# A gated recurrence followed by a rational MLP: the third pair of token groups loaded whole and turned by TensorE, with a new table of steps

## The chip, the cores and the metric

One core of a Trainium2 chip runs the whole program. The metric is the device time of one execution in microseconds (us); several executions of a kernel are timed and their median is given. A profile is one further look at one of these executions, taken by the hardware profiler. The engines are TensorE (PE in the profile; its loading of weights is PEld), VectorE (DVE), ScalarE (ACT), GpSimd (POOL) and SyncE (SP), which here only issues DMAs.

## The reference

For each of 4 batches and 8 heads there is a sequence of 768 tokens of 48 values, and a state of 48x48 that decays by `alpha` and takes up an outer product:

```python
for t in range(S):
    state = alpha[:, :, t, :, None] * state + np.einsum('bhd,bhe->bhde', k[:, :, t], v[:, :, t])
    y[:, :, t] = np.einsum('bhd,bhde->bhe', q[:, :, t], state)
x = y.transpose(0, 2, 1, 3).reshape(B * S, H * D)      # 3072 tokens of 384
h = x @ w_in                                            # 384 -> 2048
g = (a[0] + a[1]*h + a[2]*h**2 + a[3]*h**3) / (1 + |b[0]|*|h| + |b[1]|*h**2 + 1e-6)
out = g @ w_out                                         # 2048 -> 384
```

## The kernel before

**The recurrence.** The 768 tokens of a batch are worked in six groups of 128, so there are 24 groups, numbered g through all batches. Two neighbouring groups are a pair m. For each group the running products of `alpha` along the tokens are made by VectorE as two scans (`suffix` L462, `prefix` L474), k and q are multiplied by them (`mult_k` L483, `mult_q` L486, on GpSimd or VectorE), TensorE makes scores (`sc_mm` L504), turns k (`k_turn` L537), makes the products for the state (`kv_mm` L568) and the output of the group (`attn_mm` L586); GpSimd masks the scores (`sc_mask` L531) and decays the state (`decay` L556). The scans need channels on the partitions and tokens along the row, while memory holds tokens by rows, so alpha, k and q have to be turned. There are two ways of doing it.

- Groups 0 to 3 (pairs 0 and 1, `NNAT = 2`): `load_nat` (L408) loads alpha, k or q of a whole pair in one DMA of 384 KB, `turn_nat` (L425) turns it on TensorE by sixteen transposes into PSUM, and `copy_nat` (L444) has ScalarE copy it from there to where the group wants it.
- Groups 4 to 23: `load_akq` (L401) loads 48 KB at a time, 24 DMAs to a group, and VectorE turns them in 32x32 blocks (`turn_a` L454, `turn_qk` L459).

**The MLP.** Its work is cut into 96 units u: the first 8 with whole f32 weights (`plain_in` L668, `plain_out` L681), the rest as "wide" units of 128 hidden channels by 512 tokens, where weights and data are split in a high and a low part (`wide_in` L695, `wide_out` L714, and L708 for the last 512 tokens). Each unit passes through ScalarE (L750, L753, L780, L783, L799), VectorE (L773, L777, L787, L790, L796) and GpSimd (L762, L803, and L757 where ScalarE's L759 does not do that step). The weights come as 64-bit words; in the first part of the program sixteen pieces of them are brought to f32 by `join_scale` (L270, ScalarE or GpSimd), `join_low` (L278, VectorE), `join_sign` (L282 on ScalarE or L284 on VectorE) and `join` (L298, VectorE), and split by L313 and L318.

**The order.** Every step is declared once with `add(key, engine, ..., after=[...])`, the engine it runs on, an `alt` engine for some, and the steps that must stand ahead of it. `Plan.run` then issues the steps in the order of the table `ORDER`, a packed list of step numbers; the top bit of a number says that the step runs on its `alt` engine. So one table sets the order on all engines and on the DMA queue of SP, and who does the steps that two engines can do. `warm` (L418) is a row of transposes at the start that write nothing of use. At the end `last_done` (L741, L743) copies the last 512 tokens' results from PSUM in pieces of 128 tokens, and `last_store` (L747) stores them; the last 128 tokens are cut in two halves of columns, one for VectorE and one for ScalarE.

## Time and profile before

| what | us |
|---|---|
| median of 3 executions | 530.17 (528.98 to 531.47) |
| the profiled execution's own time | 531.47 |
| its span, first to last instruction | 529.4 |
| busy in the span: PE / DVE / ACT / POOL | 501.9 / 494.2 / 459.1 / 423.5 |
| PE instructions / DMA packets | 5082 / 145656 |
| mean granted TensorE clock | 0.988 of full |

The profiled execution is the longest of the three; its span leaves out 2.07 us that lie around it. A busy share here is the mean over two quite different parts: a beginning in which data and weights are prepared on all engines, and a long remainder in which the units follow each other. They have to be read apart.

### The profile page before, as it was taken

How to read it: one execution, taken by the hardware profiler on the slowest of the kernel's cores; microseconds unless marked ns; L12 is line 12 of the kernel's file. 1: busy time of each engine (PE TensorE's matmuls, PEld its weight loads, DVE VectorE, ACT ScalarE, POOL GpSimd, SP SyncE). 2: the span in 40 equal slices, each digit the busy share in tenths (PEclk: the TensorE clock that was granted, in tenths of full speed). 3: DMA queues.
4: the chain of work that ended last, by engine and by line, in shares of the span. 5: the costliest groups of instructions: out<-in, count | busy, mean ns of one | idle time of the engine just before them, and what ended most of it. 6: DMA issues, size and time to landing. Idle time of an engine off the chain costs nothing.

```text
span 529.4 us, 13659 instructions
## 1 busy us (share of the span) xinstructions
PE 501.9 (95%) x5082; PEld 411.9 (78%) x5082; DVE 494.2 (93%) x773; ACT 459.1 (87%) x805; POOL 423.5 (80%) x421
## 2 busy tenths in 40 slices
PE   7865988987999999999999999999999999999996
...
GB/s 262 248 250 268 155 197 88 106 152 132 127 144 117 89 105 100 97 99 94 119 86 116 111 91 100 83 113 32 120 83 130 47 2 41 0 61 59 2 2 63
DMA packets 145656, 56.81 MB, mean 107 GB/s; under 512 B 133424, under 2 KB 138160, under 8 KB 145584
## 3 DMA queue, kind: packets, MB, share of 16 engines
...
HBM read 47.98 MB, written 4.72 MB: 100 GB/s over the span
## 4 chain that ended last, share of the span: by engine, by line
PE 81%; ACT 6%; DVE 4%; SPq 4%; DMA 3%; issue 1%; POOL 1%; DVEq 0%; POOLq 0%
PE ps L695 34%; PE ps L714 28%; PE ps L708 6%; PE ps L586 4%; PE ps L681 2%; PE ps L504 2%; PE ps L568 2%; SPq L408 2%; PE ps L537 1%; DMA wi_words<-in_moe_w_in_dram 1%; ACT wo_words L282 1%; DMA wo_words<-in_moe_w_out_dram 1%; PE ps L668 1%; SPq L448 1%; SPq L401 1%
## 5 line engine op out<-in xcount | busy, mean ns | idle before, releaser
L695 PE MATMUL ps<-x,wi 128*128 128x512 f32 x792 | 204.4, 398 | 1.7 <-DVE t L796 1.7
L695 PEld LDWEIGHTS ps<-x,wi 128*128 128x128 f32 x792 | 146.5, 188 | 34.7 <-DVE t L796 2.7
L714 PE MATMUL ps<-gh_gl,wo 128*128 128x512 f32 x648 | 170.2, 399 | 0.2 <-ACT gh_gl L799 0.2
L714 PEld LDWEIGHTS ps<-gh_gl,wo 128*128 128x128 f32 x648 | 119.1, 188 | 27.2 <-ACT gh_gl L799 0.6
L762 POOL TENSOR_TENSOR qm<-qm,ah 128x512 f32<-128x512 f32 x96 | 124.2, 1294 | 14.8 <-ACT qm L759 5.9
L803 POOL TENSOR_TENSOR gh_gl<-t,gh_gl 128x512 fp32r<-128x512 f32 x83 | 108.6, 1309 | 16.3 <-ACT gh_gl L799 11.8
L753 ACT ACTIVATE t<-ps,coef 128x512 f32<-128x512 f32 x96 | 74.7, 778 | 6.9 <-PE ps L695 4.8
L787 DVE SCALAR_TENSOR_TENSOR t<-t,coef,ps 128x512 f32<-128x512 f32 x96 | 70.7, 737 | 6.5 <-ACT ps L783 5.1
L780 ACT ACTIVATE ps<-qm,one_eps 128x512 f32<-128x512 f32 x96 | 66.4, 691 | 11.5 <-DVE t L777 6.1
L750 ACT ACTIVATE ah<-ps 128x512 f32<-128x512 f32 x96 | 57.0, 594 | 20.6 <-PE ps L695 19.4
L777 DVE SCALAR_TENSOR_TENSOR t<-t,coef,ps 128x512 f32<-128x512 f32 x96 | 70.9, 739 | 1.0
L757 POOL TENSOR_SCALAR qm<-ah,bab 128x512 f32<-128x512 f32 x61 | 47.9, 786 | 28.6 <-ACT ah L750 16.8
L773 DVE TENSOR_TENSOR t<-t,ps 128x512 f32<-128x512 f32 x96 | 64.9, 677 | 4.6 <-ACT t L753 2.9
L796 DVE SCALAR_TENSOR_TENSOR t<-ps,t 128x512 f32<-128x512 f32 x96 | 65.6, 683 | 1.1
L790 DVE SCALAR_TENSOR_TENSOR ps<-qm,ps 128x512 f32<-128x512 f32 x96 | 65.9, 687 | 0.2
L783 ACT ACTIVATE ps<-ps 128x512 f32<-128x512 f32 x96 | 56.1, 585 | 2.0
L799 ACT ACTIVATE gh_gl<-t 128x512 fp32r<-128x512 f32 x88 | 55.1, 627 | 3.0 <-DVE t L796 2.8
L531 POOL TENSOR_SCALAR_AFFINE_SELECT tqk<-tqk 64x512 f32<-64x512 f32 x48 | 33.1, 690 | 13.9 <-ACT tqk L525 7.6
L486 POOL TENSOR_TENSOR tqk<-tqk,fp 128x512 f32<-128x512 f32 x22 | 28.9, 1312 | 8.9 <-DVE wi_words L298 7.7
L462 DVE TENSOR_TENSOR_SCAN tg<-ta,ps 128x528 f32<-128x528 f32 x24 | 29.7, 1242 | 6.6 <-ACT ta L444 6.5
L586 PEld LDWEIGHTS ps<-tqk,sv 128*32 128x32 f32 x1536 | 23.4, 112 | 15.1 <-POOL tqk L531 7.1
L483 POOL TENSOR_TENSOR tqk<-tqk,tg 128x512 f32<-128x512 f32 x23 | 30.4, 1322 | 5.6 <-ACT tqk L444 5.3
(112 smaller groups left out, 728.8 us busy)
## 6 DMA issues: line engine op xcount, KB each, us to landing
raw_a<-in_alpha_dram SPq DMA_DIRECT2D x160, 48.0 KB, 2.2
...
```

The lines of the kernel that those rows point to most:

```text
L695: nc.tensor.matmul(h_of(u), w(key)[:, kt * FU + f % FU, :], x[:, kt, xp, :], start=(n == 0), stop=(n == len(todo) - 1),)
L714: nc.tensor.matmul(bank(O_BANKS[dt]), w(("o", f // FU))[:, f % FU, dt * P : (dt + 1) * P], g, start=(f == 0 and first_w), stop=(f == NF - ...
L750: nc.scalar.activation(buf(s, "ah", u), h_of(u), AF.Abs)
L753: nc.scalar.activation(buf(s, "t1", u), h_of(u), AF.Identity, bias=a2, scale=a3)
L762: nc.gpsimd.tensor_tensor(buf(s, "qm", u), buf(s, "qm", u), buf(s, "ah", u), op=ALU.mult)
L773: nc.vector.tensor_tensor(t, t, h_of(u), op=ALU.mult)
L777: nc.vector.scalar_tensor_tensor(t, t, a1, h_of(u), op0=ALU.add, op1=ALU.mult)
L780: nc.scalar.activation(h_of(u), buf(s, "qm", u), AF.Abs_reciprocal_sqrt, bias=one_eps)
L787: nc.vector.scalar_tensor_tensor(t, t, a0, h_of(u), op0=ALU.add, op1=ALU.mult)
L790: nc.vector.scalar_tensor_tensor(h_of(u), buf(s, "qm", u), 1.0 + 1e-6, h_of(u), op0=ALU.add, op1=ALU.mult)
L796: nc.vector.scalar_tensor_tensor(t, h_of(u), 2.0, t, op0=ALU.subtract, op1=ALU.mult, reverse0=True)
L803: eng.tensor_tensor(buf(s, "gl", u).rearrange("p a b -> p (a b)"), buf(s, "t1", u), gh, op=ALU.subtract)
```

## The change

The third pair (groups 4 and 5) goes the way of the first two: `NNAT = 3`. Its alpha is loaded into the buffer that pair 0 used and its k and q into a buffer of their own (`nat_raw`), and its transposes write to PSUM bank 4 (`SCB`), which the recurrence uses as well, so they may only stand between two groups (`NAT_AFTER`: alpha behind group 2, k and q behind group 3), and one half of a pair's tensor has to be copied out before the next is turned. Since the buffers are shared, the small loads of alpha of group 6 wait for the turning of the third pair's alpha. `warm` is two products of 128x512 in place of twenty transposes. The last 128 tokens are copied by ScalarE in one piece and stored by one DMA that ScalarE issues. The table `ORDER` is another one throughout, and with it the engine of some sixty of the steps that two engines can do.

```diff
--- before.py
+++ after.py
@@ -70,70 +70,70 @@
 
 
 ORDER = [
-    'c-jTQ1E3u`3;@t3X_~gPZQHhO+qS*k?fK2NZQHhO+xFi-XN*!Rx^gOtLN!)RQeLr&t;VUzDykZ<jGCubs3|I%TBxR~`D&t',
+    'c-jru1A`sR4gk<eGRdH}ZQHhO+qT==-R-KjZQHhO+qS>HcmBmuDyl-|R2;=BiW;M0t4V6C8m~loHBK#8Q`IUpMa5FlR7^E',
...
 ]
@@ -148,8 +148,9 @@
     (0, "a"): (0, 1), (0, "k"): (4, 5), (0, "q"): (6, 7),
     (1, "a"): (0, 1), (1, "q"): (6, 7), (1, "k"): (2, 6),
 }
-NNAT = 2
-WARM = 20
+NNAT = 3
+NAT_AFTER = {"a": 2, "k": 3, "q": 3}
+WARM = 2
 WB = 2
 GB = 3
 NSC = 1
@@ -406,16 +407,22 @@
     def load_nat(m, nm):
         b, sg = divmod(m, NSEG)
         nc.sync.dma_start(
-            raw[nm][m][:, 0 : H * 2 * D].rearrange("p (h w) -> p h w", h=H),
+            raw[nm][nat_raw(m, nm)][:, 0 : H * 2 * D].rearrange("p (h w) -> p h w", h=H),
             SRC[nm][b, :, sg * SEG : (sg + 1) * SEG, :].rearrange("h (p t) d -> p h (t d)", t=2),
         )
 
     def nat_bank(m, nm, par):
-        return NAT_BANKS[m, nm][par]
+        return NAT_BANKS[m, nm][par] if (m, nm) in NAT_BANKS else SCB
+
+    def nat_raw(m, nm):
+        return m if m < 2 else 0 if nm == "a" else 2
 
     def warm():
         for n in range(WARM):
-            nc.tensor.transpose(bank(2, P), ident, ident)
+            nc.tensor.matmul(
+                bank(2).rearrange("p (a b) -> p a b", b=P), ident, ident.unsqueeze(1).to_broadcast([P, BANK // P, P]),
+                start=True, stop=True,
+            )
 
     def turn_nat(m, nm, par):
         for a in range(NPAIR):
@@ -423,7 +430,7 @@
                 c0 = 2 * D * (2 * a + j) + D * par - DP * j
                 w = DP * (j + 1)
                 nc.tensor.transpose(
-                    bank(nat_bank(m, nm, par))[0:w, a * C : (a + 1) * C], raw[nm][m][:, c0 : c0 + w], ident
+                    bank(nat_bank(m, nm, par))[0:w, a * C : (a + 1) * C], raw[nm][nat_raw(m, nm)][:, c0 : c0 + w], ident
                 )
 
     def turned(nm, g):
@@ -735,16 +742,16 @@
                 parts[32 * a : 32 * (a + 1), dt * SUP : (dt + 1) * SUP].rearrange("j (c i) -> j c i", i=32),
             )
 
-    def last_done(eng, tt, c0, c1):
-        o, x = parts[:, tt * DM + c0 : tt * DM + c1], bank(T_BANKS[tt], DM)[:, c0:c1]
+    def last_done(eng, tt):
+        o = parts[:, tt * DM : (tt + 1) * DM]
         if eng is nc.scalar:
-            eng.activation(o, x, AF.Copy)
+            eng.activation(o, bank(T_BANKS[tt], DM), AF.Copy)
         else:
-            eng.tensor_copy(o, x)
-
-    def last_store(eng, tt, c0, c1):
+            eng.tensor_copy(o, bank(T_BANKS[tt], DM))
+
+    def last_store(eng, tt):
         r = (NSUP - 1) * SUP + tt * P
-        eng.dma_start(out[r : r + P, c0:c1], parts[:, tt * DM + c0 : tt * DM + c1])
+        eng.dma_start(out[r : r + P, :], parts[:, tt * DM : (tt + 1) * DM])
 
     def act_ah(u, s):
         nc.scalar.activation(buf(s, "ah", u), h_of(u), AF.Abs)
@@ -962,7 +969,7 @@
     add("ident", "POOL", 0.5, make_identity, (nc, ident))
     add("coef", "SP", 2 * DMA, load_coef, kb=0.1)
     if WARM:
-        add("warm", "PE", 0.11 * WARM, warm, (), ["ident"], lat=0.13)
+        add("warm", "PE", 0.93 * WARM, warm, (), ["ident"], lat=0.13)
     add("bab", "ACT", 0.2, abs_coef, (), ["coef", "prime"])
     add("floor_s", "POOL", 0.1, nc.gpsimd.memset, (floor_s, FLOOR))
     add("one_eps", "POOL", 0.1, nc.gpsimd.memset, (one_eps, 1.0 + 1e-6))
@@ -1003,15 +1010,27 @@
 
     NGC = 2 * NBLK
     nat_users = [[] for _ in range(8)]
+    def cps(m, nm, par=(None, 0, 1)):
+        return [("cp", m, nm, p, cc) for p in par for cc in range(2)]
+
+    def group_done(g):
+        return [(x, g) for x in ("xh", "xl", "km", "kv")] + [("se", g, 0), ("se", g, 1)]
+
     for m in range(NNAT):
-        for nm in "aqk":
-            add(("nat", m, nm), "SP", DMA, load_nat, (m, nm), (), kb=1.45)
+        late = []
+        for nm in "aqk" if m < 2 else "akq":
+            add(("nat", m, nm), "SP", DMA, load_nat, (m, nm), [("tn", 0, nm, par) for par in range(2)] if m == 2 and nm == "a" else (), kb=1.45)
             for par in range(2):
-                b = nat_bank(m, nm, par)
-                before = [("cp", *x, p, cc) for x in nat_users[b] for p in (None, 0, 1) for cc in range(2)]
-                nat_users[b].append((m, nm))
+                if m < 2:
+                    b = nat_bank(m, nm, par)
+                    before = [y for x in nat_users[b] for y in cps(*x)]
+                    nat_users[b].append((m, nm))
+                else:
+                    before = late + group_done(NAT_AFTER[nm]) + [("kt", NAT_AFTER[nm]), ("s", NAT_AFTER[nm]), ("vk", NAT_AFTER[nm]), ("am", NAT_AFTER[nm])]
+                    late = cps(m, nm, (par,))
+                set_k = ("set", "k", nat_raw(m, "k"))
                 add(("tn", m, nm, par), "PE", 0.9, turn_nat, (m, nm, par),
-                    [("nat", m, nm), ("set", nm, m), "ident", "warm"] + before + ([("nat", m, "k"), ("set", "k", m)] if nm == "q" else []), lat=0.13)
+                    [("nat", m, nm), ("set", nm, nat_raw(m, nm)), "ident", "warm"] + before + ([("nat", m, "k"), set_k] if nm == "q" else []), lat=0.13)
     for g in range(NGC):
         m, cc = divmod(g, 2)
         old = [(w, g - NQ) for w in ("am", "s", "kt")]
@@ -1026,7 +1045,7 @@
                 ready[nm] = [("cp", m, nm, par, cc) for par in pairs]
             else:
                 for qd in range(4):
-                    ov = [("tn", 0, x, p) for p in range(2) for x in ("a" if nm == "a" else "kq") if nm == "a" or raw_at(g) == 0]
+                    ov = [("tn", y, x, p) for y in (0, 2) for p in range(2) for x in ("a" if nm == "a" else "kq") if nat_raw(y, x) == (0 if nm == "a" else raw_at(g))]
                     add(("ld", nm, g, qd), "SP", 2 * DMA, load_akq, (nm, g, qd), [("ta", g - 1) if nm == "a" else ("tqk", g - 2), ("set", nm, 0 if nm == "a" else raw_at(g))] + ov, kb=0.23)
         if m >= NNAT:
             add(("ta", g), "DVE", 0.71, turn_a, (g,), [("ld", "a", g, qd) for qd in range(4)] + into["a"])
@@ -1043,7 +1062,8 @@
             add(("sv", g, c), "SP", DMA, load_sv, (g, c), [("set", "v", g % NV), ("am", g - NV), ("vk", g - NV)], kb=0.9)
     for g in range(NGC):
         near = [("cp", *x, p, cc) for b in (SCB, SCB + 1) for x in nat_users[b] for p in (None, 0, 1) for cc in range(2)]
-        was = [("xh", g - 1), ("xl", g - 1), ("km", g - 1), ("kv", g - 1), ("se", g - 1, 0), ("se", g - 1, 1)]
+        was = group_done(g - 1)
+        near += [y for nm in "akq" if NAT_AFTER[nm] == g - 1 for y in cps(2, nm, (0, 1))]
         add(("kt", g), "PE", 0.38, k_turn, (g,), [("k", g)] + was + near, lat=0.13)
         add(("ke", g), "ACT", 0.55, k_evac, (g,), [("kt", g), ("vk", g - NSC), "set_st"])
         add(("s", g), "PE", SV[0], sc_mm, (g,), [("k", g), ("q", g), ("ke", g)] + was + near, lat=0.13)
@@ -1127,12 +1147,9 @@
                     old = [("ws", m - 1, dt) for dt in range(KT)]
                     add(("og", tt), "PE", 0.35, last_out, (u, tt, "gh"), [("gh", u), ("lo", ("o", j))] + prev, due=at)
                     add(("ot", tt), "PE", 0.175, last_out, (u, tt, "gl"), [("og", tt), ("ot", tt - 1), ("gl", u)], lat=0.13, due=at + 2)
-                    cut = DM // 2 if tt == PER - 1 else DM
-                    for c0 in range(0, DM, cut):
-                        part = (m, tt, c0) if c0 else (m, tt)
-                        act = c0 > 0 or tt == 1
-                        add(("wd", *part), "ACT" if act else "DVE", 0.5 if cut == DM else 0.33, last_done, (nc.scalar if act else nc.vector, tt, c0, c0 + cut), [("ot", tt)] + old, due=at + 3)
-                        add(("ws", *part), "ACT" if c0 else "SP", DMA, last_store, (nc.scalar if c0 else nc.sync, tt, c0, c0 + cut), [("wd", *part)], kb=0.55 * cut / DM)
+                    act, own = tt % 2, tt == PER - 1
+                    add(("wd", m, tt), "ACT" if act else "DVE", 0.5, last_done, (nc.scalar if act else nc.vector, tt), [("ot", tt)] + old, due=at + 3)
+                    add(("ws", m, tt), "ACT" if own else "SP", DMA, last_store, (nc.scalar if own else nc.sync, tt), [("wd", m, tt)], kb=0.55)
                 continue
             add(("oh", u, 0), "PE", WIDE * KT, wide_out, (u, hi, "gh"), [("gh", u), ("lo", ("o", j)), ("ol", u - 1), ("oh", u - 1, 1)] + old, due=at)
             add(("oh", u, 1), "PE", WIDE * KT, wide_out, (u, lo, "gh"), [("oh", u, 0)], due=at + 1)```

**GpSimd, groups 2 and 3, at the first units.** `tqk_88` to `tqk_90` are the buffers of turned k and q of three groups in a row: L483 and L486 with `tqk_90` and the masking with `tqk_90` belong to group 2, those with `tqk_88` to group 3; `qm` is a unit's. Before:

```order
L483 TENSOR_TENSOR tqk_90<-tqk_90,tg_86 128x512
L486 TENSOR_TENSOR tqk_88<-tqk_88,fp_85 128x512
L762 TENSOR_TENSOR qm_103<-qm_103,ah_98 128x512
L483 TENSOR_TENSOR tqk_88<-tqk_88,tg_87 128x512
L556 TENSOR_TENSOR sv_91<-st_s,tots_94 48x4x48
L556 TENSOR_TENSOR sv_91<-st_s,tg_86 48x4x48
L356 MEMSET raw_odd_82 128x48
L531 AFFINE_SELECT tqk_90<-tqk_90 64x8x64 x2
```

Now:

```order
L490 TENSOR_TENSOR tqk_90<-tqk_90,tg_86 128x512
L273 TENSOR_SCALAR parts<-wi_words 128x768
L769 TENSOR_TENSOR qm_103<-qm_103,ah_98 128x512
L764 TENSOR_SCALAR qm_104<-ah_99,bab 128x512
L769 TENSOR_TENSOR qm_104<-qm_104,ah_99 128x512
L563 TENSOR_TENSOR sv_91<-st_s,tots_94 48x4x48
L563 TENSOR_TENSOR sv_91<-st_s,tg_86 48x4x48
L62 MEMSET lim 128x1
L357 MEMSET raw_odd_82 128x48
L538 AFFINE_SELECT tqk_90<-tqk_90 64x8x64 x2
L490 TENSOR_TENSOR tqk_88<-tqk_88,tg_87 128x512
```

The product of q of group 3 (L486 with `tqk_88`) stood ahead of the decay and the masking of group 2; it is now behind them, and so is that of k of group 3. A joining of weights (L273) has come ahead.

**TensorE, from the output of group 2 on** (`x_whole` is the input of the MLP, `t_100` a unit's result). Before:

```order
L586 MATMUL ps<-tqk_90,sv_91 32x64 x32
L668 MATMUL ps<-x_whole,wi_words 128x256 x3
L537 MATMUL ps<-ident,tqk_88 128x112 x4
L668 MATMUL ps<-x_whole,wi_words 128x256 x3
L504 MATMUL ps<-tqk_88 64x64 x16
L681 MATMUL ps<-t_100,wo_words 128x256 x6
```

Now:

```order
L593 MATMUL ps<-tqk_90,sv_91 32x64 x32
L675 MATMUL ps<-x_whole,wi_words 128x256 x6
L688 MATMUL ps<-t_100,wo_words 128x256 x6
L432 MATMUL ps<-ident,raw_a_80 128x128
L432 MATMUL ps<-ident,raw_a_80 64x128
```

Group 3's turning of k and its scores stood inside the unit that follows the output of group 2; now that unit and the first output product are in one piece, and the turning of the third pair's alpha follows (eight transposes, of which two are shown), with group 3 behind it.

**VectorE, where group 4 begins** (`ta_83` is its turned alpha, `tg_86` its first scan). Before:

```order
L284 TENSOR_SCALAR wo_words<-wo_words 128x768
L454 STREAM_TRANSPOSE ta_83<-raw_a_80 128x4x2x2x32
L787 SCALAR_TENSOR_TENSOR t_100<-t_100,coef,ps 128x512
L597 TENSOR_TENSOR sv_91<-sv_91,ps 48x4x48 x2
L790 SCALAR_TENSOR_TENSOR ps<-qm_103,ps 128x512
L462 SCALAR_TENSOR_TENSOR tg_86<-ta_83,ps 128x528
L796 SCALAR_TENSOR_TENSOR t_100<-ps,t_100 128x512
```

Now:

```order
L279 TENSOR_SCALAR wo_words<-wo_words 128x768 x2
L469 SCALAR_TENSOR_TENSOR tg_86<-ta_83,ps 128x528
L285 TENSOR_SCALAR wi_words<-wi_words 128x768
L299 SCALAR_TENSOR_TENSOR wr_78<-wr_78,wo_words 128x768
L319 TENSOR_TENSOR wi_726<-wr_77,wi_726 128x6x128
L478 RECIPROCAL ta_83<-tg_86 128x4
L604 TENSOR_TENSOR sv_92<-sv_92,ps 48x4x48 x2
```

The transpose is gone from VectorE. The scan stood just ahead of the end of the first unit (L796); it now comes after that of the fourth, and beside it stand a sign step of the weights (L285) and a splitting (L319) that other engines did before.

## Rows read from the trace of the kernel before

**Rows 1.** Busy time by stretch: from, to, length, PE, PEld, DVE, ACT, POOL, clock, DMA share.

```profile
0.00:130.00 130.00, 107.14 (x1412) 89.72 (x1413) 116.50 (x176) 115.97 (x178) 86.94 (x103) 0.96 0.73 186
30.00:60.00 30.00, 21.59 (x343) 18.06 (x342) 28.02 (x43) 26.55 (x42) 18.34 (x21) 0.89 0.91 245
60.00:90.00 30.00, 26.02 (x229) 21.54 (x228) 29.42 (x47) 29.88 (x40) 18.00 (x17) 0.94 0.61 132
130.00:522.00 392.00, 392.00 (x3657) 319.79 (x3656) 375.55 (x594) 342.35 (x626) 336.61 (x319) 1.00 0.39 81
```

**Rows 2.** The same view, three stretches of 5 us.

```profile
40.00:45.00 5.00, 0.83 (x60) 0.86 (x64) 4.91 (x9) 5.00 (x6) 4.59 (x8) 1.00 0.91 233
45.00:50.00 5.00, 3.73 (x30) 2.92 (x19) 4.91 (x9) 4.00 (x6) 3.35 (x4) 0.52 1.01 292
50.00:55.00 5.00, 5.00 (x49) 4.03 (x48) 4.94 (x7) 3.72 (x8) 1.97 (x4) 0.80 1.01 284
```

**Rows 3.** Timeline of PE: start, length; in brackets idle before and what ended it.

```profile
44.17 1.10 PE L586 MATMUL ps<-tqk,sv 128*32 128x64 f32 x64 [4.21 <-POOL tqk L531]
46.54 2.93 PE L668 MATMUL ps<-x_whole,wi_words 128*128 128x256 f32 x6 [1.27 <-DVE t L796]
```

**Rows 4.** Timeline of POOL, the product of q of group 3.

```profile
36.01 1.27 POOL L486 TENSOR_TENSOR tqk<-tqk,fp 128x512 f32<-128x512 f32 x1 [7.67 <-DVE wi_words L298]
```

**Rows 5.** Timeline of PE at the start.

```profile
1.51 3.72 PE L418 MATMUL ps<-ident 128*128 128x128 f32 x20 [1.51 <-POOL ta L360]
5.07 1.91 PE L425 MATMUL ps<-ident,raw_a 128*128 128x128 f32 x16
6.82 3.66 PE L425 MATMUL ps<-ident,raw_qk 128*128 128x128 f32 x32
```

**Rows 6.** DVE groups by shape, 0 to 130 us: count, busy us, mean ns, idle before.

```profile
L459 DVE STREAM_TRANSPOSE tqk<-raw_qk 128x1024 f32<-128x1024 f32 x3 | 3.7, 1233 | 0.0
L454 DVE STREAM_TRANSPOSE ta<-raw_a 128x512 f32<-128x512 f32 x5 | 3.5, 705 | 0.0
...
L284 DVE TENSOR_SCALAR wi_words<-wi_words 128x768 uint16<-128x768 uint16 x2 | 2.1, 1070 | 0.0
...
L803 DVE TENSOR_TENSOR gh_gl<-t,gh_gl 128x512 fp32r<-128x512 f32 x2 | 1.8, 898 | 0.0
...
L547 DVE COPY tots<-tg 48x4 f32<-48x4 f32 x1 | 1.1, 1095 | 0.0
...
L483 DVE TENSOR_TENSOR tqk<-tqk,tg 128x512 f32<-128x512 f32 x1 | 0.7, 686 | 0.0
```

**Rows 7.** ACT groups by shape, 0 to 130 us, the same columns.

```profile
L282 ACT ACTIVATE wi_words<-wi_words 128x768 f16<-128x768 f32 x6 | 11.8, 1960 | 0.1
...
L270 ACT ACTIVATE parts<-wi_words 128x768 f32<-128x768 f32 x4 | 3.8, 939 | 0.0
...
L444 ACT ACTIVATE tqk<-ps 128x256 f32<-128x256 f32 x4 | 1.5, 408 | 0.0
...
L545 ACT ACTIVATE tots<-tg 48x4 f32<-48x4 f32 x5 | 1.0, 204 | 0.1
```

**Rows 8.** Line 401, small loads of alpha: min/median/max ns of one issue, first, last.

```profile
L401 SPq DMA_DIRECT2D raw_a<-in_alpha_dram x160: 311/430/2168, 17.0 to 416.6; - x160
```

**Rows 9.** Timeline of DVE, a wait for weights.

```profile
24.71 0.60 DVE L278 TENSOR_SCALAR wi_words<-wi_words 128x768 uint32<-128x768 uint32 x1 [1.26 <-DMA wi_words<-in_moe_w_in_dram]
```

**Rows 10.** Timeline of PE, two of its last waits.

```profile
122.95 0.57 PE L537 MATMUL ps<-ident,tqk 112*128 112x112 f32 x4 [1.64 <-DVE x L633]
...
129.51 2.35 PE L695 MATMUL ps<-x,wi 128*128 128x512 f32 x9 [1.08 <-DVE t L796]
```

**Rows 11.** Timeline of the end.

```profile
522.33 2.26 PE L723 MATMUL ps<-wo,gh_gl 128*128 128x384 f32 x12
...
523.93 0.49 ACT L741 ACTIVATE parts<-ps 128x384 f32<-128x384 f32 x1 [2.06 <-PE ps L723]
...
525.02 0.33 ACT L741 ACTIVATE parts<-ps 128x192 f32<-128x192 f32 x1 [0.60 <-DVE parts L743]
```

126 lines of the change are left out of this document (63 added, 63 removed).

## Prediction

> **What bounds the kernel now.** I read the busy time by stretch first. The reader is to see two parts [rows 1]. From 130 us on TensorE is busy without a gap, 392.00 of 392.00 us: there the end is set by TensorE's work alone. Before 130 us it is busy for 107.14 us, so it stands for 22.9; in the same stretch VectorE is busy for 116.50 and ScalarE for 115.97, and between 30 and 90 us VectorE has 28.02 and 29.42 of 30 us and ScalarE 29.88 of the second 30. GpSimd is the one engine with room, 86.94 of 130. So two sums decide. The time at which TensorE fills up depends on how much VectorE and ScalarE have to do before it; and since TensorE never stops afterwards, the end is TensorE's whole work plus its gaps plus what it loses at a lower clock, all of it before 130 us. A change before 130 us counts in full if it moves that sum, and not at all otherwise.
>
> Next I read where TensorE loses that time, in three stretches of 5 us and in its timeline. From 40 to 45 us it is busy for 0.83 us. It stood 4.21 us ahead of the output of group 2, until GpSimd had masked that group's scores [rows 3]. In the 5 us behind that gap the granted clock is 0.52 of full, which is all but the whole stretch at the lower of its two levels (1.2 of 2.4 GHz), and 0.80 in the next [rows 2]. Lost there: 3.73 x 0.48 + 5.00 x 0.20 = 2.8 us. A further 1.27 us ends with the last step of the first unit on VectorE. GpSimd's timeline tells why the masking was late: ahead of it in GpSimd's order stands the product of q of group 3, which had stood 7.67 us for VectorE [rows 4].
>
> **The change part by part.** *TensorE's new work.* Three tensors x two halves x eight are 48 transposes. Sixteen of the same kind start at 5.07 and are followed by the next thirty-two at 6.82 [rows 5], so 1.75 us for sixteen, 0.109 each, 5.25 us in all, at the clock that was granted there. They lie before 90 us and count in full unless a gap takes them.
>
> *The gap before the output of group 2.* In the new order GpSimd decays and masks group 2 before it touches k or q of group 3, so nothing of group 3 can hold it. What now stands ahead is a joining of weights (768 columns, one input; not shown on GpSimd before: between 1.27, the 512-column product of rows 4, and 1.5 times that) and a coefficient step, work that can start earlier. I take the 4.21 us as gone and with it the 2.8 us at the low clock; from the other side, all 7.0 stay. Of the 1.27 us I take half: VectorE's list up to that step has lost the transpose of group 4's alpha and its scan. Sum on TensorE: 5.25 - 4.21 - 2.8 - 0.6 = -2.4.
>
> *VectorE, as a check.* Gone are two turns of alpha and two of k and q, 2 x 0.705 + 2 x 1.233 = 3.9 us [rows 6]. The new table takes three more steps from it before 130 us: the product of k of group 1 (0.69), a low part of x (384 of 512 columns of that, 0.51) and a low part of a unit (0.90). It gives VectorE two sign steps (2 x 1.07 = 2.14), one splitting (768 columns, 1.03 by the product's row) and two copies of totals (0 to 1.10 each: the one shown takes 1.095, though ScalarE does the same 48x4 in 0.204 [rows 7]). Together -2.8 to -0.6. One stall of 1.26 us for weights [rows 9] may go as well, since SP now issues that piece of weights ahead of the second group's v. So -0.6 to -4.1 on the engine that feeds TensorE; the middle, -2.3, is what TensorE's own account gives.
>
> *ScalarE.* Twelve copies of 128x256 come, 12 x 0.408 = 4.9 us; two sign steps (3.9), one joining (0.94) and two totals (0.4) go [rows 7]; of the coefficient steps of the first 16 units four leave and four come. -0.4 in all: no relief.
>
> *SP.* 48 small loads go, at a median 0.43 us of issue [rows 8]: 20.6 us of SP's time. Three whole loads come; each moves what eight small ones move, so 0.43 to 3.4 us of issue. The bytes stay. Most pieces of weights now stand ahead of group 6's loads. One wait is added: the alpha loads of group 6 wait until TensorE has turned the third pair's alpha, and behind them on SP stand the whole loads of that pair's q and k, then the last weights. TensorE reaches that turn just behind the second unit's first products, the k and q turns two units later, so I cost this at nothing; if the cover is gone, each us of lateness is a us of gap.
>
> *Warming.* The twenty transposes last from 1.51 to 5.07 us [rows 5]. A product of 128x512 does not stand there; the nearest is 128x256, six records (three products) in 2.93 us at the low clock [rows 2, 3], so two of 128x512, four times the width of one, take 3.9 us at that clock and half of it at full clock: -1.6 to +0.3, and a gain ends where the first load lands. I take 0.
>
> *The end.* The last product ends at 522.33 + 2.26 = 524.59. Two half copies end at 525.02 + 0.33 = 525.35; one whole copy by ScalarE takes 0.49 [rows 11], so it ends at 525.08: -0.27, and the store follows on the same engine as before.
>
> Sum: -2.4 - 0.3 = **-2.7 us**. Of the profiled execution's own 531.47 (span 529.4 and 2.07 around it) that leaves 528.8; that execution is the longest of three, 1.3 above the median of 530.17, so against the median I forecast **527.5 us**. A measurement of this kernel can tell about 0.5%, or 2.65 us, from no change: the forecast lies on that line. Its own range is 526 to 529.5.
>
> **The rivals.** *TensorE pays for the turning (slower).* TensorE's account loses 5.25 us and need not get them back: the turns of k and q come at 60 to 75 us, where it is nearly always busy, and if q and k land late behind SP's new wait it even stops for them. The Trainium skill, page "VectorE: DVE Perf Modes", section "Rules for kernel authors", holds that for a turn within 32x32 blocks VectorE is the fastest, which speaks against this change. By that rule the program ought to be longer by what TensorE has to do in place of VectorE. The rows bear the rule out for the work itself: per pair 3.9 us on VectorE, against 5.25 on TensorE and 4.9 on ScalarE. What speaks against it as a forecast of time is that VectorE is full there and TensorE stands. It decides from the point where gaps and low clock before 130 us shrink by less than 5.25 us. With all of them left: +5.25 - 0.3 = +5.0, 535.1 us; with half of the 7.0 gone, +1.4, 531.6.
>
> *ScalarE holds it (no change).* ScalarE is at 29.88 of 30 us between 60 and 90 us and is relieved by 0.4 alone. If the units wait there, TensorE's gaps move instead of going: -0.4 - 0.3 = -0.7, 529.5 us. For it: those 30 us. Against it: ScalarE still has 14 us free before 130.
>
> *The beginning closes up further (faster).* If TensorE's late waits go too, 1.64 and 1.08 us [rows 10], because loads and weights of the groups behind come earlier by SP's 20 us: -2.7 - 2.7 = -5.4, 524.8 us. Against it: VectorE is full there whatever SP does.
>
> That the third pair is not turned on TensorE at all can't be: the order shows it.
>
> **How the numbers follow.** The forecast gets 0.44, ScalarE 0.22, the closing up 0.16, TensorE paying 0.18. The range reaches down past the closing up and up to where TensorE paying has half of its holes back and some more: 523.8 to 532.8. Faster by over 0.5% are the closing up (0.16) and rather more than half of the forecast (0.26), 0.42; slower by over 0.5% most of TensorE paying, 0.16; the rest, 0.42, lies within.
>
> **What would show it.** Right: TensorE's wait ahead of the output of group 2 under 1 us and no stretch near 0.5 of the clock behind it; TensorE's gaps before it fills up some 6 to 8 us fewer while its work rises by 5; no VectorE turns for groups 4 and 5; the last copy 0.3 us earlier. Wrong: gaps and low clock in the first 130 us that add up to as much as before, a wait of the new transposes for their load, or a gap of TensorE behind 130 us.

## The result and the profile after

| | kernel before | changed kernel |
|---|---|---|
| median of 6 executions, us | 530.16 (528.98 to 531.47) | 533.27 (532.35 to 534.60) |
| ratio, 95% interval | | 1.0062 (1.0041 to 1.0083) |
| the profiled execution's own time, its span | 531.47, 529.4 | 533.54, 531.8 |
| busy PE / DVE / ACT / POOL | 501.9 / 494.2 / 459.1 / 423.5 | 508.5 / 493.8 / 467.2 / 421.6 |

The change makes the kernel 0.6% slower, 3.1 us, where 2.7 us less were forecast. In the two profiled executions, of which that of before is the longest of its six, the difference is 2.4 us of span: TensorE's busy time grows by 508.5 - 501.9 = 6.6 and its idle time falls from 27.5 to 23.3, by 4.2.

Busy time by stretch in the changed kernel (from, to, length, PE, PEld, DVE, ACT, POOL, clock, DMA share, GB/s), the lines that answer to [rows 1]:

```profile
0.00:130.00 130.00, 112.33 (x1378) 92.72 (x1378) 113.74 (x170) 112.98 (x180) 87.33 (x101) 0.95 0.64 179
30.00:60.00 30.00, 23.73 (x291) 20.95 (x280) 28.64 (x39) 26.67 (x42) 20.93 (x19) 0.94 0.62 209
60.00:90.00 30.00, 26.56 (x248) 21.99 (x246) 27.10 (x41) 27.89 (x45) 15.56 (x16) 0.94 0.57 138
...
130.00:523.00 393.00, 391.60 (x3711) 319.32 (x3712) 377.32 (x595) 352.49 (x638) 333.57 (x316) 1.00 0.38 80
```

TensorE is busy for 5.2 us longer before 130 us, and its gaps there shrink from 22.9 to 17.7 us. Behind 130 us, where it had no gap (392.00 of 392.00 us), 1.40 us of gap have come. VectorE and ScalarE are the ones to look at: from 60 to 90 us, where they had 29.42 and 29.88 of 30 us, they now have 27.10 and 27.89. The engines that feed the units stand more there than before.

The same view in stretches of 5 us, answering to [rows 2]:

```profile
20.00:25.00 5.00, 3.66 (x78) 3.33 (x77) 4.75 (x6) 4.35 (x10) 0.98 (x2) 0.72 0.86 301
25.00:30.00 5.00, 5.00 (x63) 4.88 (x66) 4.37 (x10) 3.69 (x5) 2.59 (x3) 0.60 1.02 326
45.00:50.00 5.00, 4.44 (x72) 3.76 (x73) 4.96 (x9) 4.39 (x6) 3.56 (x4) 0.66 0.76 268
...
70.00:75.00 5.00, 5.00 (x16) 4.12 (x17) 3.33 (x5) 3.34 (x5) 3.88 (x4) 0.66 0.48 151
```

In these two executions the low granted clock has not gone but moved. By the prediction's sum (busy time times what is missing to 1.00) TensorE loses 1.0 + 2.0 + 1.5 + 1.7 = 6.2 us in these four. From 70 to 75 us VectorE and ScalarE have two thirds of a stretch each.

TensorE's timeline of the changed kernel (start, length; idle before and what ended it), answering to [rows 3]:

```profile
24.39 5.12 PE L675 MATMUL ps<-x_whole,wi_words 128*128 128x128 f32 x24
...
45.56 1.54 PE L593 MATMUL ps<-tqk,sv 128*32 128x64 f32 x64 [3.14 <-POOL tqk L538]
...
50.91 2.75 PE L688 MATMUL ps<-t,wo_words 128*128 128x256 f32 x12
53.49 1.04 PE L432 MATMUL ps<-ident,raw_a 128*128 128x128 f32 x8
54.37 2.76 PE L688 MATMUL ps<-t,wo_words 128*128 128x256 f32 x12
56.96 1.04 PE L432 MATMUL ps<-ident,raw_a 128*128 128x128 f32 x8
57.83 2.76 PE L688 MATMUL ps<-t,wo_words 128*128 128x256 f32 x12
60.43 0.55 PE L544 MATMUL ps<-ident,tqk 112*128 112x112 f32 x4
...
67.52 1.10 PE L593 MATMUL ps<-tqk,sv 128*32 128x64 f32 x64 [1.18 <-ACT wo L314]
69.86 7.13 PE L675 MATMUL ps<-x_whole,wi_words 128*128 128x256 f32 x24 [1.25 <-ACT x_whole L625]
```

and, of the same steps before,

```profile
49.26 0.95 PE L537 MATMUL ps<-ident,tqk 112*128 112x112 f32 x4
...
57.94 1.10 PE L586 MATMUL ps<-tqk,sv 128*32 128x64 f32 x64
...
60.37 2.75 PE L668 MATMUL ps<-x_whole,wi_words 128*128 128x256 f32 x12
```

The gap ahead of group 2's output is 3.14 us instead of 4.21, and ends with the same step, GpSimd's mask. Behind that output three units' output products (L688) and the turns of the third pair's alpha (L432) now stand ahead of group 3. Its key turn, at 49.26 before, starts at 60.43; its output, at 57.94 before, at 67.52. The first products of units 4 and 5, which need group 3 and began at 60.37, begin at 69.86.

GpSimd's timeline tells why the gap is still there:

```profile
31.73 1.43 POOL L633 TENSOR_TENSOR x<-x_whole,x 128x384 fp32r<-128x384 f32 x1 [3.54 <-ACT x L629]
...
35.00 2.87 POOL L273 TENSOR_SCALAR parts<-wi_words 128x768 f32<-128x768 f32 x1
...
44.13 1.37 POOL L538 TENSOR_SCALAR_AFFINE_SELECT tqk<-tqk 64x512 f32<-64x512 f32 x2
```

The product of q that had stood 7.67 us [rows 4] no longer stands ahead of the mask. But the low part of x of group 1 (L633), a step of VectorE before, is now one of GpSimd's. It waits 3.54 us for ScalarE's rounding of that group's copy (late by the products at the low clock, 5.12 us for 24), and from its start at 31.73 GpSimd works without a wait up to the mask at 44.13. In this series the joining of weights takes 2.87 us where 1.3 to 1.9 were reckoned.

The 7.67 us of before were for the most part no wait for data, as VectorE's timeline of the kernel before shows:

```profile
29.36 1.25 DVE L474 TENSOR_TENSOR_SCAN fp<-ta,ps 128x528 f32<-128x528 f32 x1
...
34.99 0.93 DVE L298 SCALAR_TENSOR_TENSOR wi_words<-parts,wi_words 128x768 uint32<-128x768 uint32 x1
```

The product of q needs this scan, which ended at 30.61 us, and copies that had ended by 23; it was released when the joining of weights (L298) ended at 35.92. `Plan.run` sets such waits: the GpSimd step that the table has next behind a VectorE step declared with `lock` (L278, L298 and a few others) is made to wait for it. So the table decides these waits of GpSimd as well.

### The profile page after: what moved, and what is told of

Its sections match the earlier page's. It is cut to its first block, busy times and chain, and to the rows that moved or that the text cites. A ratio compares the mean times of both kernels' runs of the same rounds, so it can differ in the third digit from the quotient of the medians.

```text
span 531.8 us, 13652 instructions
## 1 busy us (share of the span) xinstructions
PE 508.5 (96%) x5114; PEld 416.0 (78%) x5114; DVE 493.8 (93%) x770; ACT 467.2 (88%) x820; POOL 421.6 (79%) x416
## 4 chain that ended last, share of the span: by engine, by line
PE 73%; ACT 11%; DVE 7%; POOL 5%; issue 3%; DMA 0%; SPq 0%; POOLq 0%; ACTq 0%; DVEq 0%
PE ps L702 29%; PE ps L721 24%; PE ps L593 3%; PE ps L715 3%; PE ps L511 2%; PE ps L688 2%; PE ps L675 2%; PE ps L575 2%; ACT ps L787 1%; PE ps L544 1%; POOL qm L769 1%; ACT tqk L532 1%; PE ps L432 1%; DVE t L794 1%; ACT ps L790 1%
## 5 line engine op out<-in xcount | busy, mean ns | idle before, releaser
L769 POOL TENSOR_TENSOR qm<-qm,ah 128x512 f32<-128x512 f32 x96 | 124.4, 1296 | 19.1 <-ACT qm L766 5.8
L787 ACT ACTIVATE ps<-qm,one_eps 128x512 f32<-128x512 f32 x96 | 66.3, 691 | 14.2 <-DVE t L784 7.9
L803 DVE SCALAR_TENSOR_TENSOR t<-ps,t 128x512 f32<-128x512 f32 x96 | 65.9, 686 | 1.3
L757 ACT ACTIVATE ah<-ps 128x512 f32<-128x512 f32 x96 | 57.0, 594 | 8.4 <-PE ps L702 5.8
L790 ACT ACTIVATE ps<-ps 128x512 f32<-128x512 f32 x96 | 56.0, 584 | 2.3
L764 POOL TENSOR_SCALAR qm<-ah,bab 128x512 f32<-128x512 f32 x53 | 41.7, 788 | 17.6 <-ACT ah L757 12.3
L538 POOL TENSOR_SCALAR_AFFINE_SELECT tqk<-tqk 64x512 f32<-64x512 f32 x48 | 31.5, 655 | 10.4 <-ACT tqk L532 5.3
L490 POOL TENSOR_TENSOR tqk<-tqk,tg 128x512 f32<-128x512 f32 x24 | 32.3, 1344 | 5.5 <-ACT tqk L451 5.3
L469 DVE TENSOR_TENSOR_SCAN tg<-ta,ps 128x528 f32<-128x528 f32 x24 | 29.9, 1245 | 6.9 <-ACT ta L451 6.8
L766 ACT ACTIVATE qm<-ah,bab 128x512 f32<-128x512 f32 x43 | 34.9, 812 | 0.3
L493 POOL TENSOR_TENSOR tqk<-tqk,fp 128x512 f32<-128x512 f32 x23 | 30.5, 1326 | 4.6 <-DVE wo_words L299 3.5
```

The costliest lines, as they stand in the source:

```text
L769: nc.gpsimd.tensor_tensor(buf(s, "qm", u), buf(s, "qm", u), buf(s, "ah", u), op=ALU.mult)
L787: nc.scalar.activation(h_of(u), buf(s, "qm", u), AF.Abs_reciprocal_sqrt, bias=one_eps)
L790: nc.scalar.activation(h_of(u), h_of(u), AF.Square)
L803: nc.vector.scalar_tensor_tensor(t, h_of(u), 2.0, t, op0=ALU.subtract, op1=ALU.mult, reverse0=True)
```

## Where the difference lies in the traces

Three marks can be read in every trace: ScalarE's copy of a group out of PSUM, the first step of a unit on ScalarE and its last on VectorE. For group 1, group 3 and unit 4 these are, before,

```profile
28.71 0.49 ACT L618 ACTIVATE x_whole<-ps 128x384 f32<-128x384 f32 x1 [0.82 <-PE ps L586]
...
59.11 0.49 ACT L618 ACTIVATE x_whole<-ps 128x384 f32<-128x384 f32 x1
...
63.57 0.59 ACT L750 ACTIVATE ah<-ps 128x512 f32<-128x512 f32 x1
...
75.92 0.65 DVE L796 SCALAR_TENSOR_TENSOR t<-ps,t 128x512 f32<-128x512 f32 x1
```

and in the changed kernel

```profile
30.60 0.49 ACT L625 ACTIVATE x_whole<-ps 128x384 f32<-128x384 f32 x1 [1.86 <-PE ps L593]
...
69.32 0.49 ACT L625 ACTIVATE x_whole<-ps 128x384 f32<-128x384 f32 x1
...
74.44 0.60 ACT L757 ACTIVATE ah<-ps 128x512 f32<-128x512 f32 x1 [1.66 <-PE ps L675]
...
81.64 0.69 DVE L803 SCALAR_TENSOR_TENSOR t<-ps,t 128x512 f32<-128x512 f32 x1
```

Group 3 is 10.2 us late, unit 4 begins 10.9 us late and ends 5.8 us late. The table takes the same marks (the fourth, fifth, sixteenth and ninety-first row of a unit's last step on VectorE) from the traces of the kernels below, in us; the runs' numbers are those of the next section.

| trace | group 1 copied at | from there to end of unit 3 | of unit 4 | of unit 15 | unit 15 to 90 | unit 90 to end of span |
|---|---|---|---|---|---|---|
| before | 29.2 | 38.7 | 47.4 | 114.2 | 358.9 | 27.1 |
| run 2, no third pair | 29.0 | 38.1 | 46.8 | 113.2 | 359.1 | 27.0 |
| run 11, new start, old rest | 30.1 | 38.4 | 47.1 | 113.4 | 359.3 | 27.1 |
| run 15, old, gap filled | 29.4 | 36.4 | 44.9 | 111.2 | 359.5 | 27.1 |
| run 13, old first, new late | 29.3 | 37.8 | 46.5 | 112.8 | 362.1 | 27.6 |
| changed | 31.1 | 30.0 | 51.2 | 116.5 | 356.5 | 27.7 |
| run 4, few turns | 30.1 | 31.3 | 51.0 | 116.3 | 357.4 | 27.7 |
| run 9, start filled | 29.4 | 30.2 | 51.2 | 116.5 | 356.4 | 27.7 |
| run 16, gaps filled | 29.5 | 30.9 | 50.6 | 115.9 | 356.6 | 27.7 |
| run 10, old start, new rest | 31.6 | 31.2 | 50.9 | 116.3 | 356.8 | 27.3 |
| run 14, new first, old late | 28.3 | 31.4 | 51.1 | 115.7 | 359.8 | 27.3 |

Counted from the copy of group 1, every kernel here with the new order between 32 and 143 us ends unit 3 some 5 to 9 us earlier and unit 4 some 3 to 6 us later than every kernel with the old one, whatever its start, its clock and its turns are. Unit 15 ends 1.5 to 5.3 us later. The new order gets 2.4 us back between units 15 and 90, but only where its own first part went ahead (run 13: 362.1), and ends 0.6 us longer.

From the copy of group 1 to the end of the span the new order takes 500.2 to 501.4 us in these traces, the old one 497.8 to 500.2; runs 13 and 14, which change from one to the other near unit 15, take 502.5 and 502.8. In the two profiled executions that is 500.7 against 500.2, so that of their 2.4 us 1.9 lie at the start and 0.5 behind it. These are single executions, and that of before is the longest of its six. When group 1 is copied differs by execution rather than by order: at 28.3 us in run 14, which has the new start, and at 31.6 in run 10, which has the old one. Whether the start or the rest carries the difference of the medians the crossed runs have to tell.

## The experiments

The ratio is to the kernel before, timed beside it on the same chip (there its median was 529.11 to 530.53 us), with its 95% interval; it can differ by 0.1% from the quotient of the two medians. Where only the table of steps differs, the edit is given as the steps that move, on the engine named.

**Run 1: the third pair in the old order.** The changed code, its alpha turned behind group 3.

```diff
-NAT_AFTER = {"a": 2, "k": 3, "q": 3}
+NAT_AFTER = {"a": 3, "k": 3, "q": 3}
 table: that of before, the third pair's loads, turns and copies put in behind group 3,
 two sign steps of weights on VectorE instead of ScalarE
```

> The third pair is turned by TensorE, warming and the end are those of the change, but the table of steps is the old one with the third pair put in behind group 3 (alpha, k and q all after group 3). If the new table is to blame (group 3 issued behind the units' output products, so that units 4 and 5 start 10 us late): 527.5 to 530, no slower than before. If TensorE has to pay for the 48 transposes whatever the order: 3 to 5 us above before, 533 to 535. If SP's wait for the third pair's alpha is to blame: it does not stand in this order, so 528 to 530 as well.

Measured: 542.15 us, 1.0226 (1.0194 to 1.0257). Group 3 is copied in time, but the placing by hand makes waits of its own: TensorE stands 5.19 us at 92.80 for a unit's last step, VectorE 3.7 us for a weight and ScalarE 3.5 us for VectorE. It tells nothing on the change.

**Run 2: warming and end alone.**

```diff
-NNAT = 3
+NNAT = 2
 table: that of before, without the second half copy at the end
```

> Old table, no third pair; only the two wide warming products and the end by ScalarE alone. All theories: -0.3 us from the end and nothing from the warming, 529.5 to 530.2.

Measured: 530.13 us, 1.0004 (0.9986 to 1.0023). Two wide products and the single copy make no difference that can be told.

**Run 3: the kernel before with 48 idle turns.**

```diff
+    def idle_turns():
+        for n in range(16):
+            nc.tensor.transpose(bank(SCB, P), ident, ident)
 table: one such step inside the first products of each of units 4, 5 and 6
```

> The kernel before with 48 transposes of no use added on TensorE, 16 each inside units 4, 5 and 6, behind group 3 and ahead of group 4; nothing else is moved and nothing is taken from VectorE. If TensorE has to pay for the transposes: +4.5 to +5.3 us, about 535. If the beginning is bound by what feeds TensorE and the new table is to blame: +0 to +2, at most 532.

Measured: 535.16 us, 1.0105 (1.0079 to 1.0131). In the old order 48 turns cost 5.5 us, all of their 5.25.

**Run 4: the changed kernel without most turns.** 42 of the 48 turns are left out, so groups 4 and 5 are computed from other data.

```diff
-        for a in range(NPAIR):
-            for j in (1, 0):
+        for a in range(1 if m == 2 else NPAIR):
+            for j in (1,) if m == 2 else (1, 0):
```

> The changed kernel with 42 of the third pair's 48 transposes left out (groups 4 and 5 are computed from wrong data, everything else runs as it is). If TensorE has to pay for the transposes: -4.6 us, 528.7. If the new table is to blame: -1.0 to 0, 532.3 to 533.3, since group 3 and units 4 and 5 stay where they are in the order but for 1.8 us of transposes ahead of group 3.

Measured: 533.47 us, 1.0075 (1.0053 to 1.0097), as slow as with them. From 60 to 90 us TensorE, rid of its turns, simply stands:

```profile
60.00:90.00 30.00, 22.87 (x254) 18.10 (x255) 28.96 (x43) 28.91 (x46) 17.20 (x17) 1.00 0.58 141
```

22.87 us instead of 26.56. So in the new order the turns lie in TensorE's gaps, and TensorE's work isn't what holds it. VectorE and ScalarE have 28.96 and 28.91 of these 30 us, more than with the turns (27.10 and 27.89), and the time is the same: how much they stand here does not by itself set it either. The third pair's copies on ScalarE and its use of bank 4 are left in.

**Run 5: group 3 brought forward in the new order.**

```diff
-NAT_AFTER = {"a": 2, "k": 3, "q": 3}
+NAT_AFTER = {"a": 3, "k": 3, "q": 3}
 table, TensorE:
-output of group 2, units 3, out 0, turn alpha, out 1, turn alpha, out 2, group 3, in 4, in 5
+output of group 2, unit 3 with group 3 and out 0, 1 among it, in 4, turn alpha, turn alpha, out 2, 3, in 5
 table, other engines: group 3's and unit 4's steps ahead of the alpha copies
```

> The changed kernel with group 3 of the tokens brought forward by hand: its key turn, scores, state and output stand again among the first output products, as in the kernel before, and the alpha turns of the third pair follow it instead of standing ahead of it; copies, masks and high parts on the other engines are moved along. The rest of the new order stays. If the lateness of group 3 (its rounded copy 10 us late in the changed kernel, units 4 and 5 with it) is what costs, the copy ends near 60 us again and the time falls by 2 to 4 us against the changed kernel's 533.3, to 529.5 to 531.5. If the low clock at 20 to 30 us or SyncE's 15 us stand are what costs, or if all new orders of this part merely trade one wait for another, the time stays within 0.8 us of 533.3, or above it.

Measured: 538.93 us, 1.0175 (1.0154 to 1.0196). Group 3 is copied at 61.1 us and unit 4 begins at 65.57, as meant. But unit 4 then ends 57.6 us behind the copy of group 1, not 47: GpSimd's order had kept a weight's low part ahead of that unit's square, and in this trace GpSimd stood 14.07 us for it.

```profile
78.49 1.82 POOL L317 TENSOR_TENSOR wo<-wr,wo 128x768 fp32r<-128x768 f32 x1 [14.07 <-ACT parts L269]
```

A step that I had not moved along took the place of the one that I had. The run does not decide.

**Run 6: the same, with SyncE's loads ahead.** The edits of runs 5 and 7 together.

> As the run before, and SyncE issues the whole q and k loads of the third pair and the last two weight pieces ahead of the four alpha loads of group 6, so that they don't stand behind the wait for the third pair's alpha turns. If group 3 alone costs, the time is that of the run before, within 0.8 us. If SyncE's stand costs as well (loads of third q and k, 15 us later than they could be), it is 1 to 2 us under the run before. Neither: near 533.3.

Measured: 539.43 us, 1.0188 (1.0164 to 1.0212): as run 5, so SyncE doesn't count there either.

**Run 7: SyncE's loads ahead, alone.**

```diff
 table, SyncE:
-alpha 6, k 6, whole q of pair 3, whole k of pair 3, alpha 6, w(o,7), ..., w(i,7)
+whole q of pair 3, whole k of pair 3, w(o,7), w(i,7), alpha 6, k 6, alpha 6, ...
```

> The changed kernel with the one edit on SyncE: the third pair's whole q and k loads and the last two weight pieces are issued ahead of group 6's alpha loads. If SyncE's stand of 15 us behind that wait is what makes the change slow, the time falls by 2 us or more, to 531 or less. If the lateness of group 3 or the start is, it stays within 0.8 us of 533.3, since the q and k turns of the third pair wait for nothing in the trace.

SyncE's wait behind the turning of alpha, from the waits up to 150 us (engine, line, waited for: us in total, times, longest), in the changed kernel:

```profile
SPq L402 <- PE ps L432: 17.5, 2, 15.1
```

and in this one:

```profile
SPq L400 <- PE ps L430: 8.9, 2, 6.5
```

The longest wait is less than half as long, and the span is 531.9 us against 531.8, with every mark within 0.2 us of the changed kernel's. So a wait of SyncE that is 8.6 us shorter gains nothing in the span. The time, 537.06 us, 1.0149 (1.0123 to 1.0175), is neither what one theory nor what the other expected: here 5.2 to 5.8 us lie around the span, where it is 1.7 to 2.1 in the other kernels. Where these come from no view shows.

**Run 8: idle turns at the start.** Forty turns into bank 3.

```diff
+        for n in range(8):
+            nc.tensor.transpose(bank(3)[:, 384:512], ident, ident)
 table, TensorE: five times, between 13 and 22 us
```

> The changed kernel with 40 idle turns of the identity (5 times 8, some 0.9 us each at the full clock) set where TensorE waits between 13 and 22 us; nothing reads them. If the granted clock at 20 to 30 us (0.72 and 0.60 in the changed kernel, 1.00 before) costs the 2 to 3 us, it is back near 1.00 there, the first 24 products of unit 0 and 1 take 2.8 to 3.0 us instead of 5.1, and the time falls by 1.5 to 2.5 us, to 531 to 532. If group 3's lateness is the cause, the 2.2 us won at 24 to 30 us are lost again in the wait ahead of group 2's output, which grows, and the time stays within 0.8 us of 533.3. If the fillers delay what follows, it rises by up to 2 us.

Measured: 539.20 us, 1.0182 (1.0152 to 1.0212). The first of them waited for VectorE's scan, which reads its floor from the same bank:

```profile
17.46 1.09 PE L427 MATMUL ps<-ident 128*128 128x128 f32 x8 [3.06 <-DVE tg L471]
```

Not a test of the clock. But group 0 is copied 3.9 us later than in the changed kernel and the span is 5.1 us longer: here lateness at the start is not taken in later.

**Run 9: the same into free banks.** 24 turns into banks 7 and 0, where TensorE waits.

> The changed kernel with 24 idle turns of the identity (3 times 8) ahead of group 0's output, group 1's key turn and group 1's scores, where TensorE waits 1.24, 1.06 and 1.34 us; they go to banks 7 and 0, which nothing uses just then (the earlier try wrote to bank 3, where VectorE reads its floor, and so made a wait of its own). If the low granted clock behind these waits is what costs, the first 24 products of units 0 and 1 take 2.8 to 3.0 us instead of 5.1, and the time falls by 1.5 to 2.3 us against the changed kernel, to 531 to 531.8. If not, it stays within 0.8 us of 533.3.

TensorE's timeline, the first products of units 0 and 1:

```profile
24.27 2.94 PE L677 MATMUL ps<-x_whole,wi_words 128*128 128x128 f32 x24
```

In the trace the clock from 20 to 30 us is 1.00, the 24 products take 2.94 us instead of 5.12, group 1 is copied 1.7 us earlier, and the span, 530.0, is 1.8 shorter. That execution, 531.72 us, is the fastest of six: the median is 533.66, 1.0081 (1.0051 to 1.0111). So in one execution of each the full clock at the start goes with 1.8 us, which may be chance as well, and the median isn't lower for it.

**Runs 10 and 11: crossed at 32 us.**

```diff
 run 10, table: the first 123 steps of the old order, then the new one (changed code)
 run 11, table: the first 127 steps of the new order, then the old one (code of before)
```

> The changed kernel's code, with the old order for the first 123 steps (to the rounding of group 1 and the first products of units 0 and 1, some 32 us) and the new order for all that follows; the third pair is turned on TensorE as in the change. If the beginning of the new order costs (the low clock at 20 to 30 us, group 1's copy 1.9 us later), the copy of group 1 ends at 29.2 again and the time is 530.5 to 531.5. If the late group 3 and what follows it cost, it stays within 0.8 us of 533.3.

> The other way round: the kernel before, with the new order for the first 127 steps and the old one for all that follows; groups 4 and 5 as before. If the new beginning costs, group 1's copy ends near 31.1 instead of 29.2 and the time rises by 1 to 2 us, to 530.5 to 532. If the rest of the new order costs, the time is that of the kernel before, 529.1 to 530.2.

Measured: run 10 532.53 us, 1.0060 (1.0033 to 1.0087); run 11 530.49 us, 1.0010 (0.9992 to 1.0029). The loss goes with the rest of the order, not with its start. Two things limit this: run 11 has no third pair on TensorE, so what goes with the rest may be its order or the third pair, and in run 10's traced execution group 1 is copied at 31.6 us and not at 29.2, though it has the old start.

**Run 12: group 3 early and all steps up to unit 13 in another order,** with another engine for 27 of them and alpha turned behind group 3 (`NAT_AFTER` as in run 5).

> The changed kernel with group 3 brought forward as in the run that came out 10 us too slow, but with all steps from the beginning to unit 13 put in another order by hand and search, so that unit 4's square on GpSimd no longer stands behind a weight's low part (there GpSimd stood 14 us). If the late group 3 is what the new order costs, the copy of group 3 ends at 52 to 56 us, and the time falls below the kernel before, to 525 to 529. If the third pair on TensorE costs in any order, it stays at 531 or above.

Measured: 548.27 us, 1.0362 (1.0335 to 1.0388), with waits on all engines; the copy of group 3 ends at 62.8 us, not at 52 to 56. A miss: it says nothing on the late group 3.

**Runs 13 and 14: crossed near unit 15.**

```diff
 run 13, NNAT = 2, table: the old order to unit 18, then the new one
 run 14, table: the new order to unit 14, then the old one (third pair as in the change)
```

> The changed kernel's code without the third pair (groups 4 and 5 turned on VectorE), with the old order up to the last step of unit 18 (some 158 us) and the new order for all that follows. In the traces the new order takes 356.5 us from the end of unit 15 to that of unit 90 where the old one takes 358.9, and ends 0.6 us longer behind unit 90. If the whole loss lies before unit 15, and the late part of the new order is worth 1.8 us by itself, the time is 527 to 528.5. If the new order is only faster late because it is behind early (work that it has put off is not missing), it is 529.7 within 0.8.

> The changed kernel with its third pair, with the new order up to the last step of unit 14 (some 143 us) and the old order for all that follows. If the loss lies early and the late part gains, the 4.2 us by which unit 15 is late are kept and the time is 533.5 to 535, at or above the changed kernel. If the old late order takes the lateness in, it is 529.5 to 531.

Measured: run 13 531.91 us, 1.0030 (1.0004 to 1.0055); run 14 534.51 us, 1.0091 (1.0062 to 1.0120). Runs 11 and 14 both have the new start and the old late part, and between them lies 0.8%: this puts the loss between 32 and 143 us, where the third pair's turns and copies lie too. The late part of the new order gains nothing by itself. Run 13 is 0.3% slower although it has the old order there, with 362.1 us from unit 15 to unit 90, so a crossing can have a price of its own.

**Runs 15 and 16: the gap ahead of group 2's output filled,** in the kernel before (30 turns into bank 7) and in the changed one (20 turns, and 30 at the start in the places where run 9 had 24).

```diff
+        for n in range(10):
+            nc.tensor.transpose(bank(b)[:, 0:128], ident, ident)
 table, TensorE: three times (run 16: twice) ahead of the output of group 2
```

> The kernel before, with 30 idle turns of the identity (3.3 us of TensorE's time) in the gap of 4.21 us ahead of group 2's output, into bank 7, which nothing uses there. The prediction priced the low granted clock behind this gap at 2.8 us. If that price is right, the granted clock at 45 to 55 us is near 1.00 and the time falls by 2 to 2.8 us, to 527 to 527.7. If the work behind the gap isn't held by TensorE, the clock rises and the time stays within 0.8 us of 529.7.

> The changed kernel with 50 idle turns: 30 at the beginning as in the earlier run (10 each ahead of group 0's output, group 1's key turn and its scores) and 20 in the gap of 3.14 us ahead of group 2's output. In the one traced execution of the earlier run the first products ran at the full clock and all that followed came 1.8 us earlier, but the median of its runs did not fall. If low granted clock in the first 50 us is what the changed kernel loses by, it is now 531 to 532 in the median. If it is the order itself, it stays at 533 to 534.5.

TensorE's timeline in run 15, to be held against [rows 3]:

```profile
40.01 3.44 PE L421 MATMUL ps<-ident 128*128 128x128 f32 x30
43.85 1.10 PE L589 MATMUL ps<-tqk,sv 128*32 128x64 f32 x64 [0.41 <-DVE sv L600]
```

Busy time and clock behind it, to be held against [rows 2]:

```profile
45.00:50.00 5.00, 3.33 (x20) 2.63 (x23) 4.90 (x9) 4.46 (x7) 2.88 (x4) 1.00 1.06 273
50.00:55.00 5.00, 4.99 (x81) 4.11 (x82) 4.97 (x8) 4.85 (x10) 3.85 (x5) 1.00 1.08 253
```

The idle turns take the gap, the clock behind it is 1.00 instead of 0.52 and 0.80, and in this trace unit 4 ends 2.5 us earlier behind group 1. The ratio, though, is 0.9989 (0.9971 to 1.0007), 0.6 us less with both signs inside the interval; the medians are 529.41 and 530.53 us. None of its twelve executions is above 530.4 us, where 15 of the 29 of the kernel before are. Run 16: 532.88 us, 1.0047 (1.0024 to 1.0069). Over its twelve executions the mean granted clock is 0.993 to 0.999, against 0.982 to 0.994 in the changed kernel, and it remains slower than before. With the gaps filled in both, the two kernels are 1.0047 - 0.9989, or 0.58%, apart, much as without the filling (0.62%). The low clock is not what separates them.

**Runs 17 and 18: VectorE's weight steps and GpSimd's steps kept apart.** Other tables up to unit 15, for the changed kernel and the kernel before, with another engine for 14 and 8 of the steps.

> The changed kernel with its third pair and its late group 3, with the steps up to unit 15 put in another order, in which VectorE's integer steps on weights stand where GpSimd has nothing running and the other way round; no step is added or left out. In the traces VectorE's steps of one shape take up to three times as long where a GpSimd step runs beside them (a weight's low words 0.55 us and 1.62), and GpSimd waits for VectorE's steps: the changed kernel has some 3.6 us of such stretching by 160 us, the kernel before 2.0, the slowest trial 9.4. If this is what the new order costs, the stretching falls to 1 us or less, and the time falls to 525 to 530, at or under the kernel before, with group 3's copy still near 65 to 70 us. If the late group 3 itself costs, it stays at 532 or above.

> The kernel before, without a third pair on TensorE, with its steps up to unit 15 put in another order on the same rule (VectorE's integer steps and GpSimd's steps apart). If the collisions cost, the time falls to 525 to 528.5. Beside the run above it shows what the third pair is worth when both orders are made alike: the same time within 1 us if turning on VectorE costs nothing that counts, 1.5 us or more in the other's favour if VectorE's 3.9 us count.

Measured: run 17 540.85 us, 1.0197 (1.0167 to 1.0227); run 18 547.43 us, 1.0321 (1.0289 to 1.0352). By the length of each VectorE step above the median of its line and shape, summed to 160 us, the stretching fell from 5.5 to 3.1 us and from 4.0 to 2.1, not to 1 or less as was meant. Both became much slower by waits between engines: GpSimd's masks alone stood 14.3 us in six waits for ScalarE in run 17. Neither shows a cause or a better version.

## Why the prediction was wrong, step by step

- **The step that failed** is "I take the 4.21 us as gone and with it the 2.8 us at the low clock". Of the gap 3.14 us stayed: what now stands ahead on GpSimd was called "work that can start earlier", but the low part of x, which the prediction took from VectorE and did not count on GpSimd, stands ahead of it and waits for group 1's copy, and the joining was sized 1.3 to 1.9 us and took 2.87. The low clock stayed as well: 0.66 behind the gap, and 0.60 to 0.72 in three other stretches. The step also looked at one gap for the whole stretch and did not follow what was put behind: group 3's turn 11 us later, units 4 and 5 with it.
- In TensorE's account of the two profiled executions the clock is the term that missed. Gaps before 130 us fell by 5.2 us, where 4.8 were reckoned, but at the two places named only by 2.3 (4.21 to 3.14, and the 1.27 gone), and 1.4 us of gap came behind 130 us, a sign of being wrong that the prediction had named. The low clock was to take 2.8 us less; by the prediction's sum over all stretches of 5 us before 130 us it takes 6.3 in place of 4.1.
- But that account does not give the time. In run 2's traced execution, with the old order, the same sum is 6.1 us, 2.0 more than before, and the span is 528.3 us, 1.1 less. The 2.8 us were not far from what one filled execution shows (run 15: 529.22 us against 531.47), but are 0.6 us by the ratio, with an interval on both sides of nothing.
- TensorE's new work was priced rightly, 5.25 us (run 3: 5.5), and counted in full in the sum, though "unless a gap takes them" stood beside it. In the new order the gaps take them (run 4).
- VectorE's check came out inside its bounds, -2.8 us before 130 us (113.74 against 116.50 [rows 1]), and gave no time. Some of that is luck: over the whole span VectorE has only 0.4 us less (493.8 against 494.2). And from 70 to 75 us it waits, 3.33 of 5 us busy, so less work there gains nothing.
- ScalarE was reckoned at -0.4 us; before 130 us it has 3.0 less and over the span 8.1 more (467.2 against 459.1): the table gives it eight more coefficient steps that GpSimd had, 43 of 0.81 us instead of 35, and moves others behind 130 us.
- SyncE's added wait, costed at nothing, came (15.1 us); cut to 6.5 it leaves the span as it was (run 7). Warming and the end, 0 and -0.3, can't be told from nothing (run 2); behind unit 90 the new order ends 0.6 us longer.
- The rival on the slower side gave 531.6 to 535.1, and 533.27 was measured, but not by its mechanism: leaving the turns out gains nothing. The rule of the Trainium skill that this rival named (page "VectorE: DVE Perf Modes", section "Rules for kernel authors") has VectorE as the fastest for a turn within 32x32 blocks. The rows agree, with 3.9 us of VectorE's time against 5.5 us of the kernel's in run 3, and run 4 shows that the time need not follow.

What is shown: by the ratios of the crossed runs the loss goes with what the change does between 32 and 143 us, and it doesn't go away without most of the third pair's turns, with less than half of SyncE's longest wait, or with the clock at 0.993 and above; the start of the new order adds at most 0.3% (run 11). Not tested is the new order there without the third pair's copies on ScalarE and its turns in bank 4, so order and third pair can't be told apart beyond the turns themselves. In size the two readings agree loosely at best: behind the copy of group 1 the traced executions with the new order take 0.2 to 2.0 us longer than those with the old one (filled gaps and runs 13 and 14 left out), and the ratios of runs 10 and 11 are 0.5% or 2.6 us apart. Within that stretch the traces show the new order falling behind between the ends of units 3 and 4: the alpha turns and three units' output products stand ahead of group 3, so unit 4 begins 10.9 us later, and VectorE and ScalarE stand from 70 to 75 us. That the late group 3 alone is the cause is argued from that place and not shown: the trials that brought it forward (runs 1, 5, 6 and 12) all made waits of their own. No trial beats the kernel before by more than can be measured; run 15 comes nearest.
